# Turned activation blocks sent through DRAM, turns ordered behind residual sums, and a last output tile computed by halves, in a four-layer attention/MLP kernel

## The chip, the cores and the metric

The kernel runs on one core of one Trainium2 chip. The metric is device microseconds of one execution. The kernel before takes 790.73 us (median of three runs: 789.31, 790.73, 791.21).

## The reference, cut to what matters

Four layers run one after the other on the same rows x (2048 tokens of D = 576 features), with the weights of A used twice and those of B used twice:

```
x = A_x
x = x + _A_ref(_layernorm(x), A_wqkv, A_wo)                    # layer 0
x = x + _B_ref(_layernorm(x), B_w1, B_b1, B_w2, B_b2)          # layer 1
x = x + _A_ref(_layernorm(x), A_wqkv, A_wo)                    # layer 2
x = x + _B_ref(_layernorm(x), B_w1, B_b1, B_w2, B_b2)          # layer 3

_A_ref: q,k,v = x@wqkv (32 heads of 18);  pq, pk = phi(q), phi(k);  kv = pk^T v;  z = sum pk
        o = (pq kv) / (pq z + 1e-6);  return o @ wo
_B_ref: y = _layernorm(x);  h = gelu(y@w1 + b1)  (4608 wide);  return h@w2 + b2
```

`_B_ref` normalizes its input once more; the kernel folds the two normalizations into one factor.

## The kernel before, in words

Tokens are cut into 16 tiles of 128 (`t`) and four chunks of 512 (`c`, four tiles each). Every projection wants the normalized rows with features on partitions, so the kernel keeps one big tile `yT` (128 partitions x 5 blocks of features x 2048 tokens): the last block is half full, and for the MLP its 64 rows are there twice, because the MLP works on the two halves of TensorE's rows at once.

**The way into `yT`.** Class `LNPipe` moves one token tile one stage further at each `tick()` (L255): load the rows from the DRAM copy `x_d` into one of two buffers (L265), statistics (L272, L273), `rstd` on GpSimd (L288), normalize into one of three `y_ring` buffers (L307), for the MLP copy the 64 tail columns once more (L311, GpSimd), then turn. Tiles of layer 0 and the first chunk of each MLP are turned on TensorE into a PSUM bank (`tp`, L322 to L328). All others go through `turn_rows` (L221): VectorE turns 32x32 blocks into the one buffer `turned` (L225), which holds the four tiles of a chunk, and after the fourth tile 16 DMAs of 40 or 32 KB each carry the blocks into `yT`, issued from SyncE's queue (L232). The next chunk's first turn overwrites `turned`, so it waits until those DMAs have landed.

**The MLP** (`LayerB.run`, L646). For each chunk: nine groups of the first matmul (`m1_group`, L583; 36 PSUM results through gelu on ScalarE), during which the four tiles of the next chunk are fed to the pipe (`feed_next`, L649); then for each of the four token tiles 72 matmuls of the second projection into one of two PSUM accumulators, `accA` and `accB` (L672), and a residual sum on VectorE (L379) that also frees the accumulator. The first projection of a chunk needs its columns of `yT`. In layer 1 each finished tile is fed to the pipe again, for layer 2. `feed_next` holds loads and statistics behind the last residual sum only for the first chunk.

**The attention layers** (`layer_A`, L388): k and v per tile, q per group of heads and chunk; then denominators (L496, with a one-row matmul that adds epsilon, L500), the scaling (L512 to L515) and the output projection (L523), with the same residual sum.

**What sets the order.** TensorE's order in the program is written out by hand (`pe`, L137). On VectorE, GpSimd and the DMA queue of SyncE a scheduler places the instructions by their dependencies; edges marked NOSYNC only say what stands behind what on one engine. Each engine then works strictly in that order, and an instruction that waits holds all behind it. PSUM has eight banks: three for the pool `ps_h`, one for `tp`, two for each accumulator.

Of the kernel before, what the change touches and what calls it, by code (L numbers as in the profile page):

```python
# [8 lines left out]
ALU = mybir.AluOpType  # L9
BF16 = mybir.dt.bfloat16  # L10
F32 = mybir.dt.float32
PSUM = bass.MemoryType.PSUM
# [3 lines left out]
P = 128  # L16
NT = S // P
KD = 5
# [16 lines left out]
def build(tc, A_x, A_wqkv, A_wo, B_w1, B_b1, B_w2, B_b2, out, dbg=None, n_layers=4):  # L35
    nc = tc.nc
    dbg = dbg or {}
    with ExitStack() as ctx:
        const = ctx.enter_context(tc.tile_pool(name="const", bufs=1))
        ps_h = ctx.enter_context(tc.tile_pool(name="ps_h", bufs=3, space=PSUM))  # L40
        ps_tp = ctx.enter_context(tc.tile_pool(name="ps_tp", bufs=1, space=PSUM))
        ps_acc = ctx.enter_context(tc.tile_pool(name="ps_acc", bufs=1, space=PSUM))
        dpool = ctx.enter_context(tc.tile_pool(name="dram", bufs=1, space=DRAM))

# [172 lines left out]
        state = dict(ycnt=0, vcnt=0, xl=0)  # L217
        pool_last = dict(norm=None)
        dve_last = dict(norm=None, sum=None, phi=None)

        def turn_rows(y, t, kind):  # L221

            c, j = divmod(t, TPC)
            nb = 4 * KD if kind == "B" else D // 32
            nc.vector.transpose(out=turned[:, 0:nb, j, :], in_=y[:, 0:32 * nb])  # L225
            if j < TPC - 1:
                return
            for i in range(4):
                for jj in range(4):
                    nk = KD if 16 + jj < nb else KD - 1  # L230
                    cols = slice(c * CB + i * P, c * CB + (i + 1) * P)
                    nc.sync.dma_start(  # L232
                        out=yT[32 * jj:32 * (jj + 1), 0:nk, cols],
                        in_=turned[32 * i:32 * (i + 1), jj:4 * (nk - 1) + jj + 1:4].rearrange("p k t c -> p k (t c)"))

        def spread(ap):

# [5 lines left out]
        class LNPipe:  # L243
# [9 lines left out]
                return len(self.items)  # L253

            def tick(self, transposes=1):  # L255
                for it in list(self.items):
                    st = it["stage"]
                    if st == 4 and it["evac"] != "dma":
# [27 lines left out]
                    elif st == 1:  # L286
                        rstd = work.tile([P, 1], F32, name="ln_rstd", bufs=6)
                        nc.gpsimd.tensor_tensor(out=rstd[:], in0=it["u"][:], in1=neg_half[:], op=ALU.pow)  # L288
                        it["rstd"] = rstd
                    elif st == 2 and it["norm"] != "dve":  # L290
                        nmr = work.tile([P, 1], F32, name="ln_nmr", bufs=4)
                        nc.gpsimd.tensor_scalar(out=nmr[:], in0=it["mv"][:, 0:1], scalar1=-1.0,
                                                scalar2=it["rstd"][:, 0:1], op0=ALU.mult, op1=ALU.mult)
                        it["nmr"] = nmr
                    elif st in (2, 3):
                        y = y_ring[state["ycnt"] % NY]
                        state["ycnt"] += 1
                        xt = it["xt"]
                        if it["norm"] == "act":
                            nc.scalar.activation(out=y[:, 0:D], in_=xt[:, 0:D], func=ACT.Identity,  # L300
                                                 scale=it["rstd"][:, 0:1], bias=it["nmr"][:, 0:1])
                        elif it["norm"] == "pool":
                            norm = nc.gpsimd.tensor_scalar(out=y[:, 0:D], in0=xt[:, 0:D], scalar1=it["rstd"][:, 0:1],
                                                           scalar2=it["nmr"][:, 0:1], op0=ALU.mult, op1=ALU.add)
                            pool_last["norm"] = norm.ins.name
                        else:
                            norm = nc.vector.tensor_scalar(out=y[:, 0:D], in0=xt[:, 0:D], scalar1=it["mv"][:, 0:1],  # L307
                                                           scalar2=it["rstd"][:, 0:1], op0=ALU.subtract, op1=ALU.mult)
                            dve_last["norm"] = norm.ins.name
                        if it["kind"] == "B":  # L310
                            nc.gpsimd.tensor_copy(out=y[:, D:DPAD], in_=y[:, 4 * P:D])  # L311
                        it["y"] = y
                        it["stage"] = 4
                        continue
                    elif st == 4:
                        y = it["y"]
                        t = it["t"]
                        if it["evac"] == "dma":
                            turn_rows(y, t, it["kind"])
                            self.items.remove(it)  # L320
                            continue
                        tp = ps_tp.tile([P, KD, P], BF16, name="tp", tag="tp")  # L322
                        for k in range(KD):
                            pe(nc.tensor.transpose(out=tp[:, k, :], in_=y[:, k * P:(k + 1) * P], identity=ident[:]))
                        if it["evac"] == "act":
                            nc.scalar.copy(out=yT[:, :, t * P:(t + 1) * P], in_=tp[:])
                        else:
                            nc.vector.tensor_copy(out=yT[:, :, t * P:(t + 1) * P], in_=tp[:])  # L328
                        self.items.remove(it)
                        continue  # L330
                    it["stage"] = st + 1

            def drain(self):
                while self.items:
                    self.tick()

        lnp = LNPipe()
# [34 lines left out]
        def residual(li, t, halves):  # L372
            xo = xo_of.pop((li, t))
            last = (li == n_layers - 1)
            if last:
                xn = work.tile([P, 2 * D], BF16, name="xbf", tag="xn", bufs=3)[:, 0:D]
            else:
                xn = work.tile([P, D], F32, name="xn", tag="xn", bufs=3)[:]
            total = nc.vector.tensor_tensor(out=xn.rearrange("p (h n) -> p h n", h=2), in0=halves,  # L379
                                            in1=xo.rearrange("p (h n) -> p h n", h=2), op=ALU.add)  # L380
            dve_last["sum"] = total.ins.name
            if last:
                nc.sync.dma_start(out=out_f[t * P:(t + 1) * P, :], in_=xn)
                return None
            nc.sync.dma_start(out=x_d[t], in_=xn)
            return xn
# [188 lines left out]
        class LayerB:  # L575
# [70 lines left out]
            def run(self):  # L646
                li, next_kind = self.li, self.next_kind

                def feed_next(c, i):  # L649
                    if c + 1 < NCB:  # L650
                        t = (c + 1) * TPC + i
                        lnp.feed(None, t, "B", "dve", "dma", load_from=t, after=(dve_last["sum"] if c == 0 else None))

                for c in range(NCB):
                    for g in range(self.done.get(c, 0), NGRP):
# [11 lines left out]
                    for j in range(TPC):  # L667
                        t = c * TPC + j
                        acc = ps_acc.tile([P, 2, 512], F32, name="m2_ps", tag=next_acc())
                        for f in range(NF):  # L670
                            for half in range(2):
                                pe(nc.tensor.matmul(acc[:, half, 0:HALF], lhsT=hT[f][:, j * P:(j + 1) * P],  # L672
                                                    rhs=w2_sb[:, f, half * HALF:(half + 1) * HALF],
                                                    start=(f == 0), stop=(f == NF - 1)))
# [111 lines left out]
```

## Time and profile before

The profile is of one execution of 790.27 us; its span is 788.6 us, and 1.67 us lie around the span. Stages by the chain of waits and the timeline:

| stage | span, us | what TensorE does |
|---|---|---|
| layer 0 (attention) | 0 to 112.2 | projections to 75, scaling and output to 112 |
| layer 1 (MLP) | 112.2 to 394.0 | four times 35 us first, 35.4 us second projection |
| layer 2 (attention) | 394.0 to 491.9 | as layer 0 |
| layer 3 (MLP) | 491.9 to 784.9 | first chunk ends late, the others as in layer 1 |
| last sum and store | 784.9 to 788.6 | idle |

| engine | busy us | share of span |
|---|---|---|
| TensorE matmul | 769.9 | 98% |
| ScalarE | 341.7 | 43% |
| VectorE | 275.4 | 35% |
| GpSimd | 127.0 | 16% |

How to read the lines further below: in a timeline a line has start, length, engine, line of the kernel, operation, output<-input with shapes, how many, and in brackets the idle time before it with what ended it. "SPq" is the queue on which SyncE issues DMAs. In the list of waits the numbers are microseconds in total, times, and the longest. In the table of stretches each engine has its busy time and number of instructions; the three last columns are TensorE's granted clock (1.00 is full), the busy share of the DMA engines, and GB/s.

### The profile page before, as it was taken

The numbers are of one execution on the slowest core, as the hardware profiler recorded it, in microseconds if no ns is written. First come the engines' busy times: TensorE is split into PE (matmuls) and PEld (weight loads), VectorE is DVE, ScalarE is ACT, GpSimd is POOL, SyncE is SP. The second block draws the span as 40 slices with busy tenths as digits, with TensorE's granted clock in tenths as the row PEclk, the third lists the DMA queues.
The fourth block names the chain that finished last, engine by engine and source line by source line (L and its number), as shares of the span: only waits on it lengthen the run. The fifth ranks groups of instructions, "written<-read, shape, count | busy, mean of one in ns | idle before, by whom it ended". The sixth has DMA issues, their size and how long they took to land.

```text
span 788.6 us, 15939 instructions
## 1 busy us (share of the span) xinstructions
PE 769.9 (98%) x6613; PEld 496.5 (63%) x6613; DVE 275.4 (35%) x710; ACT 341.7 (43%) x754; POOL 127.0 (16%) x211
## 2 busy tenths in 40 slices
PE   8999999999999999999999999996999999999998
PEld 5776654675477457547777756455744764675476
DVE  6786864044324413301355597544100000000000
ACT  5888636304610650362077774650056016304600
POOL 4671403013000301200000022311110010001000
PEclk9999999999999999999999999998899999999999
DMA  9990473122412331311120028443410110011000
GB/s 265 280 294 5 130 252 91 22 75 66 94 43 69 83 65 46 91 17 31 61 61 2 1 89 288 152 94 79 86 39 1 31 61 2 5 50 38 1 24 23
DMA packets 70642, 63.23 MB, mean 80 GB/s; under 512 B 37418, under 2 KB 55210, under 8 KB 70570
## 3 DMA queue, kind: packets, MB, share of 16 engines
q1 hardware_dynamic: 70570, 62.21, 28.1%
q8 instruction: 52, 0.85, 0.4%
q14 instruction: 20, 0.16, 0.1%
HBM read 39.38 MB, written 16.52 MB: 71 GB/s over the span
## 4 chain that ended last, share of the span: by engine, by line
PE 83%; DVE 7%; DMA 4%; SPq 3%; POOL 1%; issue 1%; ACT 1%; DVEq 0%; POOLq 0%
PE m_ps L672 34%; PE h_ps L624 17%; PE hp_ps L624 14%; PE q_ps L436 5%; PE k_ps L400 5%; PE v_ps L415 3%; SPq L232 3%; PE v_ps L412 2%; PE wo_ps L523 2%; DVE xn L379 1%; DMA x_d<-xn 1%; DVE turned L225 1%; PE kvacc L430 1%; DMA x_ring<-x_d 1%; DVE y_ring L307 1%
## 5 line engine op out<-in xcount | busy, mean ns | idle before, releaser
L672 PE MATMUL m_ps<-w_sb,hT 128*128 128x288 bf16 x2304 | 286.2, 287 | 8.5 <-DVE xbf L379 8.5
L672 PEld LDWEIGHTS <-hT 128*128 128x128 bf16 x2304 | 225.9, 98 | 69.8 <-issue 12.1
L624 PEld LDWEIGHTS <-w_sb 64*128 64x128 bf16 x2304 | 124.4, 94 | 136.6 <-issue 1.9
L624 PE MATMUL hp_ps<-yT,w_sb 64*128 64x512 bf16 x1152 | 178.0, 376 | 0.0
L629 ACT COPY relay_sb<-relay_sb 128x1 f32<-128x1 f32 x144 | 28.5, 198 | 276.6 <-PE h_ps L624 234.7
L624 PE MATMUL h_ps<-yT,w_sb 64*128 64x512 bf16 x1152 | 147.9, 376 | 0.0
L620 ACT ACTIVATE hT<-h_ps,b1T 128x512 bf16<-128x512 f32 x144 | 91.2, 684 | 44.5 <-PE h_ps L624 44.5
L288 POOL TENSOR_TENSOR ln_rstd<-ln_u,neg_half 128x1 f32<-128x1 f32 x64 | 36.2, 567 | 413.9 <-DVE ln_u L281 216.8
L620 ACT ACTIVATE hT<-hp_ps,b1T 128x512 bf16<-128x512 f32 x144 | 91.2, 693 | 0.0
L379 DVE TENSOR_TENSOR xbf<-m_ps,x_ring 128x576 bf16<-128x576 f32 x16 | 12.0, 754 | 221.2 <-PE m_ps L672 221.2
L369 POOL TENSOR_TENSOR x_ring<-x_ring,b_bc 128x576 f32<-128x576 f32 x32 | 41.1, 1291 | 203.7 <-DMA x_ring<-x_d 203.6
L379 DVE TENSOR_TENSOR xn<-m_ps,x_ring 128x576 f32<-128x576 f32 x16 | 12.1, 758 | 155.9 <-PE m_ps L672 155.9
L624 PE MATMUL h_ps<-yT,w_tail 64*128 64x512 bf16 x144 | 54.1, 376 | 0.0
L624 PE MATMUL hp_ps<-yT,w_tail 64*128 64x512 bf16 x144 | 54.1, 376 | 0.0
L436 PE MATMUL q_ps<-yT,wqkv_sb 128*126 128x512 bf16 (+1 forms) x200 | 50.0, 382 | 0.5 <-ACT phi_a L351 0.5
L225 DVE STREAM_TRANSPOSE turned<-y_ring 128x640 bf16<-128x640 bf16 (+1 forms) x40 | 32.2, 812 | 41.8 <-DMA yT<-turned 35.4
L523 PE MATMUL wo_ps<-kvwo,pq 126*128 126x288 bf16 (+1 forms) x320 | 43.7, 285 | 2.1 <-DVE xn L379 1.6
L400 PE MATMUL k_ps<-wqkv_sb,yT 128*128 128x288 bf16 x320 | 44.3, 286 | 0.0
L350 ACT ACTIVATE phi_e<-k_ps 128x288 bf16<-128x288 f32 x64 | 27.0, 421 | 34.8 <-PE k_ps L400 34.7
L352 DVE TENSOR_SCALAR phi_e<-phi_e 128x288 bf16<-128x288 bf16 (+2 forms) x104 | 30.7, 296 | 25.3 <-ACT phi_e L350 24.9
L523 PEld LDWEIGHTS <-pq 126*128 126x128 bf16 (+1 forms) x320 | 30.5, 97 | 13.7 <-issue 3.9
L400 PEld LDWEIGHTS <-yT 128*128 128x128 bf16 x320 | 30.9, 98 | 11.1
(90 smaller groups left out, 625.7 us busy)
## 6 DMA issues: line engine op xcount, KB each, us to landing
x_ring<-x_d SPq DMA_DIRECT2D x72, 288.0 KB, 3.1
x_d<-xn SPq DMA_DIRECT2D x48, 288.0 KB, 2.2
w_sb<-in_B_w_dram SPq DMA_DIRECT2D x6, 864.0 KB, 9.5
yT<-turned SPq DMA_DIRECT2D x128, 40.0 KB, 2.0
w_sb<-in_B_w_dram SPq DMA_DIRECT2D x9, 512.0 KB, 5.5
x<-in_A_x_dram SPq DMA_DIRECT2D x16, 144.0 KB, 4.1
x_ring<-in_A_x_dram SPq DMA_DIRECT2D x16, 144.0 KB, 3.4
out_dram<-xbf SPq DMA_DIRECT2D x16, 144.0 KB, 1.8
```

The costliest lines, as they stand in the source:

```text
L225: nc.vector.transpose(out=turned[:, 0:nb, j, :], in_=y[:, 0:32 * nb])
L288: nc.gpsimd.tensor_tensor(out=rstd[:], in0=it["u"][:], in1=neg_half[:], op=ALU.pow)
L352: nc.vector.tensor_scalar(out=e[0:rows, 0:n], in0=e[0:rows, 0:n], scalar1=1.0, scalar2=1e-6, op0=ALU.min, op1=ALU.add)
L369: nc.gpsimd.tensor_tensor(out=xo, in0=xo, in1=b2_bc[:], op=ALU.add)
L379: total = nc.vector.tensor_tensor(out=xn.rearrange("p (h n) -> p h n", h=2), in0=halves, in1=xo.rearrange("p (h n) -> p h n", h=2), op=ALU ...
L400: pe(nc.tensor.matmul(kp[:, 0:HALF], lhsT=yT[:, k, tok], rhs=wqkv_sb[:, k, D + half * HALF: D + (half + 1) * HALF], start=(k == 0), stop=( ...
L436: pe(nc.tensor.matmul(qp[0:GR[g], :], lhsT=wqkv_sb[:, k, GO[g]:GO[g] + GR[g]], rhs=yT[:, k, c * CA:(c + 1) * CA], start=(k == 0), stop=(k ...
L523: pe(nc.tensor.matmul(wp[:, half, 0:HALF], lhsT=pq[(g, c)][0:GR[g], j * P:(j + 1) * P], rhs=kvwo[g][0:GR[g], half * HALF:(half + 1) * HALF ...
L620: act_last["gelu"] = nc.scalar.activation(out=to, in_=ps, func=ACT.Gelu_apprx_tanh, bias=b1T[:, f:f + 1], scale=1.0).ins.name
L624: mm = pe(nc.tensor.matmul(dst[n], lhsT=wt, rhs=mv, start=(seen[n] == 0), stop=(seen[n] == 8)))
L629: relay = nc.scalar.copy(out=relay_sb[:, 1:2], in_=relay_sb[:, 0:1])
L672: pe(nc.tensor.matmul(acc[:, half, 0:HALF], lhsT=hT[f][:, j * P:(j + 1) * P], rhs=w2_sb[:, f, half * HALF:(half + 1) * HALF], start=(f == ...
```

## The change

- `turn_rows` sends a full `turned` buffer to one of two DRAM buffers `y_d` by four DMAs of 32 x 18 x 128 elements (144 KB each). A list `landing` counts three ticks; then `land` reads the chunk from DRAM into `yT` by one DMA of 128 x 4 x 512 elements and one or, for the MLP, two of 64 x 512. The second of these writes the doubled tail, so the GpSimd copy is left out for these tiles, and 18 instead of 20 blocks are turned.
- Each turn is ordered behind the latest residual sum, and the loads and statistics of all chunks, not of the first alone, behind the latest residual sum at their feeding.
- `tp` has no bank of its own any more; `ps_h` has four banks, `tp` among their users.
- The epsilon matmul has 126 rows (125 of them zero) instead of one.
- The last token tile of the last layer runs its 72 matmuls half by half; the residual sum and the store of that tile are two each, of 288 columns.

```diff
-        ps_h = ctx.enter_context(tc.tile_pool(name="ps_h", bufs=3, space=PSUM))
-        ps_tp = ctx.enter_context(tc.tile_pool(name="ps_tp", bufs=1, space=PSUM))
+        ps_h = ctx.enter_context(tc.tile_pool(name="ps_h", bufs=4, space=PSUM))
...
-        eps_row = const.tile([1, H], BF16, name="eps_row")
-        one_row = const.tile([1, P], BF16, name="one_row")
+        eps_row = const.tile([126, H], BF16, name="eps_row")
+        one_row = const.tile([126, P], BF16, name="one_row")
...
-            fill(eps_row, 1e-6),
+            fill(eps_row, 0.0),
+            lambda: nc.gpsimd.memset(eps_row[0:1, :], 1e-6),
...
-        turned = const.tile([P, 4 * KD, TPC, 32], BF16, name="turned")
+        turned = const.tile([P, D // 32, TPC, 32], BF16, name="turned")
+        y_d = [dpool.tile([D // 32, 32, CB], BF16, name=f"y_d{i}") for i in range(2)]
...
         def turn_rows(y, t, kind):
             c, j = divmod(t, TPC)
-            nb = 4 * KD if kind == "B" else D // 32
-            nc.vector.transpose(out=turned[:, 0:nb, j, :], in_=y[:, 0:32 * nb])
+            turn = nc.vector.transpose(out=turned[:, :, j, :], in_=y[:, 0:D])
+            if dve_last["sum"] is not None:
+                tc.add_manual_dep(turn.ins, dve_last["sum"], NOSYNC, reason="rows are turned behind the sums")
             if j < TPC - 1:
                 return
+            home = y_d[state["turns"] % 2]
+            state["turns"] += 1
             for i in range(4):
-                for jj in range(4):
-                    nk = KD if 16 + jj < nb else KD - 1
-                    cols = slice(c * CB + i * P, c * CB + (i + 1) * P)
-                    nc.sync.dma_start(
-                        out=yT[32 * jj:32 * (jj + 1), 0:nk, cols],
-                        in_=turned[32 * i:32 * (i + 1), jj:4 * (nk - 1) + jj + 1:4].rearrange("p k t c -> p k (t c)"))
+                nc.sync.dma_start(out=home[:, :, i * P:(i + 1) * P].rearrange("j r n -> r j n"),
+                                  in_=turned[32 * i:32 * (i + 1), :, :, :].rearrange("r j t c -> r j (t c)"))
+            landing.append([3, home, c, kind])
+
+        def land(now=False):
+            for it in list(landing):
+                it[0] -= 1
+                if it[0] > 0 and not now:
+                    continue
+                _, home, c, kind = it
+                landing.remove(it)
+                cols = slice(c * CB, (c + 1) * CB)
+                nc.sync.dma_start(out=yT[:, 0:KD - 1, cols],
+                                  in_=home[0:16, :, :].rearrange("(k jj) r n -> (jj r) k n", jj=4))
+                for hi in range(2 if kind == "B" else 1):
+                    nc.sync.dma_start(out=yT[64 * hi:64 * (hi + 1), KD - 1, cols],
+                                      in_=home[16:18, :, :].rearrange("jj r n -> (jj r) n"))
...
             def tick(self, transposes=1):
+                land()
...
-                        if it["kind"] == "B":
+                        if it["kind"] == "B" and it["evac"] != "dma":
                             nc.gpsimd.tensor_copy(out=y[:, D:DPAD], in_=y[:, 4 * P:D])
...
-                        tp = ps_tp.tile([P, KD, P], BF16, name="tp", tag="tp")
+                        tp = ps_h.tile([P, 512], F32, name="tp", tag="h")
+                        tp = tp[:, 0:DPAD // 2].bitcast(BF16).rearrange("p (k n) -> p k n", k=KD)
...
+            parts = [slice(h * HALF, (h + 1) * HALF) for h in range(2)] if last and t == NT - 1 else [slice(0, D)]
+            for i, cols in enumerate(parts):
+                ps = halves if len(parts) == 1 else halves[:, i:i + 1, :]
...
+                if last:
+                    nc.sync.dma_start(out=out_f[t * P:(t + 1) * P, cols], in_=xn[:, cols])
...
-                        lnp.feed(None, t, "B", "dve", "dma", load_from=t, after=(dve_last["sum"] if c == 0 else None))
+                        lnp.feed(None, t, "B", "dve", "dma", load_from=t, after=dve_last["sum"])
...
-                        for f in range(NF):
-                            for half in range(2):
-                                pe(nc.tensor.matmul(acc[:, half, 0:HALF], lhsT=hT[f][:, j * P:(j + 1) * P],
+                        by_half = li == n_layers - 1 and t == NT - 1
+                        steps = [(f, half) for half in range(2) for f in range(NF)] if by_half else \
+                            [(f, half) for f in range(NF) for half in range(2)]
```

More of the change, by code (lines that the diff above doesn't have):

```diff
@@ L215, in build @@
                       [(lambda i=i: piece_w2(i)) for i in range(6)] + [piece_b1_dma]
-        state = dict(ycnt=0, vcnt=0, xl=0)
+        state = dict(ycnt=0, vcnt=0, xl=0, turns=0)
         pool_last = dict(norm=None)
         dve_last = dict(norm=None, sum=None, phi=None)
+        landing = []
         def turn_rows(y, t, kind):
             c, j = divmod(t, TPC)
-            nb = 4 * KD if kind == "B" else D // 32
-            nc.vector.transpose(out=turned[:, 0:nb, j, :], in_=y[:, 0:32 * nb])
+            turn = nc.vector.transpose(out=turned[:, :, j, :], in_=y[:, 0:D])
+            if dve_last["sum"] is not None:
+                tc.add_manual_dep(turn.ins, dve_last["sum"], NOSYNC, reason="rows are turned behind the sums")
             if j < TPC - 1:
                 return
+            home = y_d[state["turns"] % 2]
+            state["turns"] += 1
             for i in range(4):
-                for jj in range(4):
-                    nk = KD if 16 + jj < nb else KD - 1
-                    cols = slice(c * CB + i * P, c * CB + (i + 1) * P)
-                    nc.sync.dma_start(
-                        out=yT[32 * jj:32 * (jj + 1), 0:nk, cols],
-                        in_=turned[32 * i:32 * (i + 1), jj:4 * (nk - 1) + jj + 1:4].rearrange("p k t c -> p k (t c)"))
+                nc.sync.dma_start(out=home[:, :, i * P:(i + 1) * P].rearrange("j r n -> r j n"),
[14 more added lines that the diff above has]
+                                      in_=home[16:18, :, :].rearrange("jj r n -> (jj r) n"))
         def spread(ap):
@@ L325, in tick @@
                         if it["evac"] == "act":
-                            nc.scalar.copy(out=yT[:, :, t * P:(t + 1) * P], in_=tp[:])
+                            nc.scalar.copy(out=yT[:, :, t * P:(t + 1) * P], in_=tp)
                         else:
-                            nc.vector.tensor_copy(out=yT[:, :, t * P:(t + 1) * P], in_=tp[:])
+                            nc.vector.tensor_copy(out=yT[:, :, t * P:(t + 1) * P], in_=tp)
                         self.items.remove(it)
@@ L333, in drain @@
             def drain(self):
-                while self.items:
+                while self.items or landing:
                     self.tick()
@@ L378, in residual @@
                 xn = work.tile([P, D], F32, name="xn", tag="xn", bufs=3)[:]
-            total = nc.vector.tensor_tensor(out=xn.rearrange("p (h n) -> p h n", h=2), in0=halves,
-                                            in1=xo.rearrange("p (h n) -> p h n", h=2), op=ALU.add)
-            dve_last["sum"] = total.ins.name
+            parts = [slice(h * HALF, (h + 1) * HALF) for h in range(2)] if last and t == NT - 1 else [slice(0, D)]
+            for i, cols in enumerate(parts):
+                ps = halves if len(parts) == 1 else halves[:, i:i + 1, :]
+                nh = ps.shape[1]
+                total = nc.vector.tensor_tensor(out=xn[:, cols].rearrange("p (h n) -> p h n", h=nh), in0=ps,
+                                                in1=xo[:, cols].rearrange("p (h n) -> p h n", h=nh), op=ALU.add)
+                dve_last["sum"] = total.ins.name
+                if last:
+                    nc.sync.dma_start(out=out_f[t * P:(t + 1) * P, cols], in_=xn[:, cols])
             if last:
-                nc.sync.dma_start(out=out_f[t * P:(t + 1) * P, :], in_=xn)
                 return None
@@ L669, in run @@
                         acc = ps_acc.tile([P, 2, 512], F32, name="m2_ps", tag=next_acc())
-                        for f in range(NF):
-                            for half in range(2):
-                                pe(nc.tensor.matmul(acc[:, half, 0:HALF], lhsT=hT[f][:, j * P:(j + 1) * P],
-                                                    rhs=w2_sb[:, f, half * HALF:(half + 1) * HALF],
-                                                    start=(f == 0), stop=(f == NF - 1)))
+                        by_half = li == n_layers - 1 and t == NT - 1
+                        steps = [(f, half) for half in range(2) for f in range(NF)] if by_half else \
+                            [(f, half) for f in range(NF) for half in range(2)]
+                        for f, half in steps:
+                            pe(nc.tensor.matmul(acc[:, half, 0:HALF], lhsT=hT[f][:, j * P:(j + 1) * P],
+                                                rhs=w2_sb[:, f, half * HALF:(half + 1) * HALF],
+                                                start=(f == 0), stop=(f == NF - 1)))
+                            if half == 0:
+                                continue
                             if f % 12 == 6:
```

## The prediction

> **What bounds the kernel now.** I read the page's busy times first, then the list of waits, then the place where TensorE waits longest, engine by engine.
>
> The page, engines over the span:
>
> ```profile
> PE 769.9 (98%) x6613; PEld 496.5 (63%) x6613; DVE 275.4 (35%) x710; ACT 341.7 (43%) x754; POOL 127.0 (16%) x211
> ```
>
> TensorE has matmuls in flight all but 18.7 us, so only what it waits for can be won. The list of waits:
>
> ```profile
> DVE turned L225 <- DMA yT<-turned: 35.4, 4, 10.3
> ...
> PE m_ps L672 <- DVE xbf L379: 8.5, 1, 8.5
> ```
>
> One wait of TensorE is long: a second-projection tile waits for a residual sum. The timeline of TensorE around it:
>
> ```profile
> 526.98 17.81 PE L672 MATMUL m_ps<-w_sb,hT 128*128 128x288 bf16 x144
> 553.34 20.19 PE L672 MATMUL m_ps<-w_sb,hT 128*128 128x288 bf16 x144 [8.54 <-DVE xbf L379]
> ```
>
> Two tiles (144 matmuls) of layer 3's first chunk fill both accumulators; the third waits 8.54 us. VectorE at that time:
>
> ```profile
> 537.14 0.58 DVE L307 TENSOR_SCALAR y_ring<-x_ring,ln_mv,ln_rstd 128x576 bf16<-128x576 f32 x1 [0.67 <-POOL ln_rstd L288]
> 545.42 1.57 DVE L225 STREAM_TRANSPOSE turned<-y_ring 128x640 bf16<-128x640 bf16 x2 [7.70 <-DMA yT<-turned]
> ...
> 551.80 0.84 DVE L225 STREAM_TRANSPOSE turned<-y_ring 128x640 bf16<-128x640 bf16 x1 [0.34 <-POOL y_ring L311]
> 552.57 1.38 DVE L379 TENSOR_TENSOR xbf<-m_ps,x_ring 128x576 bf16<-128x576 f32 x2
> ```
>
> The first tile's products lay ready at 526.98 + 17.70/2 = 535.8, but the sum stands in VectorE's order behind the turning of chunk 4, which waits 7.70 us until the DMAs of chunk 3 have left `turned`. Those are slow to issue; SyncE's queue:
>
> ```profile
> 532.80 10.98 SPq L232 DMA_DIRECT2D yT<-turned  x16
> ```
>
> The stretches show the second half of the price, the clock:
>
> ```profile
> 515.00:545.00 30.00, 29.80 (x256) 19.36 (x253) 11.46 (x30) 9.97 (x22) 4.12 (x11) 1.00 0.40 82
> 545.00:560.00 15.00, 6.66 (x35) 4.49 (x35) 7.45 (x16) 0.00 (x0) 1.53 (x4) 0.66 0.29 66
> ```
>
> The granted clock is 0.66 over the stretch with the stall, 1.00 before, and the 144 matmuls behind it take 20.19 us. Undisturbed, 288 take 35.39 us in the chain of waits, so 144 take 17.70: 2.49 us are lost to the clock.
>
> **The change, part by part.** All against the profiled execution, 790.27 us (span 788.6 and 1.67 around it).
>
> 1. *The order on VectorE.* In the changed program's order of instructions, the four sums of layer 3's first chunk stand ahead of all statistics and turns of chunk 3, and those of each later chunk likewise. Only chunk 2 is turned before the first sum; before, it was done by 512.7, and the sum is due at 535.8. So the stall goes whole: −8.54 us, and −2.49 us of slow clock with it. What is late next? Behind 553 TensorE shows no wait before the end, and layer 1 has none at all, although VectorE waits there 10.30 us at 201.6 and 9.53 us at 271.2 for the same reason: the next sum was far away.
>
> 2. *The way through DRAM.* Per chunk 16 issues (10 to 11 us of queue) become 4 writes, one read and one or two tail reads. The trace has no write of 256-byte pieces into DRAM; call W the time from the first of the four issues to the last landing. From below: 288 KB of `x_d<-xn` land in 2.2 us, so 576 KB in 4.4. From above: `yT<-turned`, in equal 256-byte pieces, has 160 pieces per DMA, lands in 2.0 us and is issued every 0.65 us; the 2304 pieces at that pace take 9.4 us and a landing, 11.4; one DMA after the other, 14.4 x 2.0 = 28.8. I take W = 7 us: four issues of about 0.95 (between 0.60 for 160 pieces here and 1.12 for 768 at L196) and some 3 to land, nearer the pipelined row, since the DMAs do overlap in the trace. The read is 512 KB in 1 KB pieces like the `w_sb` loads at L188: 0.6 to issue, 5.5 to land, with the tails 6.5 us.
>
>    Is it hidden? Due times are the starts of the first projection. Layer 1, chunk 2: turned at 131.6, due 182.6. Layer 1, chunks 3 and 4 are tightest, since two sets pass one `turned`: the finished rows' writes start at 188.65, about 7 us of turning follows (201.6 to 208.9) behind their landing, then a second W and the read: 188.65 + 2W + 13.5 against 253.1, so W may be 25.5. Layer 2, tile 12: turned at 398.8, due 435.07 less 6.5: W up to 29.8. Layer 3: chunk 2 from 512.8, due about 562.4; chunks 3 and 4 are now begun only when the chunk before is summed, so load to turn some 16 us (496.9 to 512.7), then 13.5: 30 us of the 70 that a chunk lasts. At W = 7 nothing shows: 0 us. On SyncE's queue the read stands directly behind the writes and holds the queue until they have landed; behind it stand the stores and prefetches of the next chunk's sums, due at about 226 in layer 1, when the queue is free since about 216. The three ticks set program order alone.
>
> 3. *GpSimd's tail copy and two blocks less per turn.* 24 copies (0.25 us) and 24 times some 0.08 us of VectorE go, off the path: 0 us.
>
> 4. *PSUM banks and epsilon rows.* In the attention layers' output stages TensorE waits 0.5 us for a bank (q_ps on ScalarE) and 0.7 (rden_ps on VectorE); four shared banks may save up to 1.2. Four epsilon matmuls advance TensorE 0.19 us in the chain, twenty of the 126-row ones 0.40; at that pace eight groups save 8 x 0.11 = 0.9. A loss is possible where `tp` now keeps a bank of the shared four until ScalarE has copied it: I allow one more wait like that of q_ps, 0.5. In layer 0's first stage each step takes exactly four banks, so each is reused one step later, as before. These stages are VectorE's (16.1 of 17 us busy at 75 to 92), so little reaches the end: −0.3 us, between −2.1 and +0.5.
>
> 5. *The last tile by halves.* The order of matmuls changes, not their number. In the built program the first half's sum waits for TensorE's count of all 6613 matmuls, and the second sum has no wait of its own: TensorE reports once for the tile. So nothing overlaps. Now:
>
> ```profile
> 781.80 3.10 PE L672 MATMUL m_ps<-w_sb,hT 128*128 128x288 bf16 x24
> 785.00 0.76 DVE L379 TENSOR_TENSOR xbf<-m_ps,x_ring 128x576 bf16<-128x576 f32 x1 [8.06 <-PE m_ps L672]
> 785.79 0.33 SPq L383 DMA_DIRECT2D out_dram<-xbf  x1
> ```
>
>    A 288-column row of VectorE (the statistics) takes 0.46 us and starts its successor 0.37 later. The halves end at 785.46 and 785.83 instead of 785.76, and the second issue follows at about 785.9: +0.1 us. Bounds: −0.2 (half the bytes land sooner) to +0.4 (a whole issue more).
>
> Sum: 788.6 − 8.54 − 2.49 − 0.3 + 0.1 = 777.4; with 1.67 around it 779.0. The profiled run is 0.46 below the median of the runs shown, so I forecast 779.3 us, between the two readings. Its own range, from the bounds of 4 and 5 and the runs' spread: 777 to 781.
>
> **The rivals.**
>
> *Slower: the writes into DRAM run one after the other.* Two W must pass in layer 1, chunks 3 and 4; from W = 25.5 on TensorE waits at 253 and 323. At the serial bound, 28.8, each loses 2 x 3.3 = 6.6 us, and 2.5 us of clock as behind the stall here: 2 x 9.1 = 18.2, and 779.3 + 18.2 = 797.5. The gain of 11 us and 2.4 more (0.3%) are given back from 2 x (2 x (W − 25.5) + 2.5) = 13.4 on, at W = 27.6. For it: pieces of 256 bytes, no such row in the trace. Against: sixteen DMAs of such pieces overlapped in 11 us. Chance 0.04. The Trainium skill, "DMA: Bandwidth & Descriptors", sections "Specifications" and "Why small descriptors are slow (HBM only)", speaks for it: transfers under 512 bytes make the engine read, modify and write, and the penalty is on DRAM, not between on-chip memories. If that doubled the 9.4 us of pieces, W would be an estimated 21 us and the sum unchanged.
>
> *No change: the stall moves.* Layer 3's chunks 3 and 4 used to be turned by 533 and 553, 111 and 162 us ahead of their first projections (643.99, 714.45); now the work starts only 70 us ahead. If it took 75 us instead of 30, two stalls of 5 us would give back the gain: 789.3. Against: load to turn of chunk 2 took 16 us with the same instructions. That the order stays as it was is excluded by the listing. Chance 0.05.
>
> *More: part 4 reaches the end.* If its waits lie on the path, another 1.8 us: 777.2. VectorE's 95% speaks against. Chance 0.13.
>
> **How the numbers follow.** Forecast 0.78, more 0.13, stall moves 0.05, serial writes 0.04. A measurement of this kernel can tell about 0.3% (2.4 us) from no change. Faster by over that: 0.91 (the first two); within: 0.05; slower: 0.04. The range, 776.5 to 782.5, holds the first two cases and a little of a stall left over.
>
> **What would show it.** In the changed profile: no TensorE wait at L672's successor before the last sum; VectorE's waits of turns on DMAs (35.4 us) shrunk to the two in layer 1; granted clock 1.00 between 515 and 575; the last two sums both after the last matmul; first projections of layer 1 starting at 182.6, 253.1 and 323.5 as before. A first-projection matmul or a `k_ps` weight load waiting on a DMA would make the forecast wrong, and its length minus 6.5 us of reading gives W.

## The result

The changed kernel takes 778.39 us (median of four runs, 777.95 to 779.44) against 790.02 for the kernel before beside it (four runs, 789.22 to 791.21): ratio 0.9854, 95% interval 0.9835 to 0.9872. The profiled execution took 778.56 us with a span of 776.8. The forecast was 779.3 us.

The page after: engines over the span, and the granted clock of TensorE in 40 slices.

```profile
PE 766.6 (99%) x6613; PEld 495.1 (64%) x6613; DVE 273.3 (35%) x711; ACT 340.6 (44%) x754; POOL 121.4 (16%) x188
PEclk9999999999999999999999999999999999999999
```

TensorE is idle for 10.2 us instead of 18.7, and the clock never drops. The list of TensorE's waits has no row for `m_ps` any more; this is the longest that is left:

```profile
PE wo_ps L548 <- DVE xn L403: 1.8, 4, 0.9
```

The second projection of layer 3's first chunk, on TensorE's timeline, is one block of four tiles:

```profile
526.43 35.45 PE L699 MATMUL m_ps<-w_sb,hT 128*128 128x288 bf16 x288
```

VectorE at that time: the last turn of chunk 2, and behind it nothing but sums, each waiting for TensorE and not the reverse.

```profile
510.10 0.78 DVE L227 STREAM_TRANSPOSE turned<-y_ring 128x576 bf16<-128x576 bf16 x1
535.46 0.76 DVE L403 TENSOR_TENSOR xbf<-m_ps,x_ring 128x576 bf16<-128x576 f32 x1 [24.58 <-PE m_ps L699]
544.28 0.76 DVE L403 TENSOR_TENSOR xbf<-m_ps,x_ring 128x576 bf16<-128x576 f32 x1 [8.06 <-PE m_ps L699]
```

SyncE's queue: a set of four writes into DRAM, and 5.0 us after the first of them the read into `yT`.

```profile
510.91 2.44 SPq L235 DMA_DIRECT2D y_d<-turned  x4
515.92 0.38 SPq L248 DMA_DIRECT2D yT<-y_d  x1
```

The same two stretches as before the change: clock 1.00 in both, and 124 matmuls instead of 35 in the second.

```profile
515.00:545.00 30.00, 30.00 (x260) 19.81 (x255) 1.48 (x2) 9.29 (x21) 1.28 (x1) 1.00 0.14 40
545.00:560.00 15.00, 15.00 (x124) 11.97 (x123) 0.79 (x2) 0.00 (x0) 0.00 (x0) 1.00 0.13 40
```

Where the time came from, as starts on TensorE's timeline (us):

| point | before | after | gained so far |
|---|---|---|---|
| layer 1, first matmul | 112.10 | 110.77 | 1.33 |
| layer 2, first matmul | 393.84 | 392.50 | 1.34 |
| layer 3, first matmul | 491.91 | 491.36 | 0.55 |
| layer 3, second projection of its first chunk | 526.98 | 526.43 | 0.55 |
| layer 3, first projection of chunk 2 | 573.47 | 561.81 | 11.66 |
| last matmul ends | 784.90 | 773.25 | 11.65 |
| span ends | 788.57 | 776.85 | 11.72 |

Of the 11.7 us, 11.11 come from one chunk of layer 3; the rest is some half microsecond in the attention layers and 0.07 behind the last matmul. That layer 2 seems to give back 0.79 us is scatter: from its first matmul to that of layer 3 it takes 98.1 to 99.1 us in the four profiles without the new banks and epsilon rows (the kernel before and three experiments below) and 97.6 to 99.3 in the seven with both whose TensorE has no long wait in layer 1.

### The profile page after: what moved, and what is told of

Read it like the earlier page. It is cut to its first block, busy times and chain, and to the rows that moved or that the text cites. A ratio compares the mean times of both kernels' runs of the same rounds, so it can differ in the third digit from the quotient of the medians.

```text
span 776.8 us, 15765 instructions
## 1 busy us (share of the span) xinstructions
PE 766.6 (99%) x6613; PEld 495.1 (64%) x6613; DVE 273.3 (35%) x711; ACT 340.6 (44%) x754; POOL 121.4 (16%) x188
## 4 chain that ended last, share of the span: by engine, by line
PE 91%; DVE 3%; DMA 2%; POOL 1%; ACT 1%; issue 1%; SPq 0%; DVEq 0%; POOLq 0%; ACTq 0%
PE m_ps L699 36%; PE h_ps L649 20%; PE hp_ps L649 16%; PE k_ps L425 5%; PE q_ps L461 5%; PE v_ps L440 3%; PE v_ps L437 2%; PE wo_ps L548 2%; DVE xn L403 1%; DMA x_d<-xn 1%; PE kvacc L455 1%; DMA wqkv_sb<-in_A_wqkv_dram 1%; POOL y_ring L322 1%; PE tp L344 1%; DMA x<-in_A_x_dram 0%
## 5 line engine op out<-in xcount | busy, mean ns | idle before, releaser
L403 DVE TENSOR_TENSOR xbf<-m_ps,x_ring 128x576 bf16<-128x576 f32 (+1 forms) x17 | 12.2, 721 | 218.5 <-PE m_ps L699 218.5
L649 PEld LDWEIGHTS <-w_tail 64*128 64x128 bf16 x288 | 27.1, 94 | 17.1
```

The lines of the kernel that those rows point to most:

```text
L403: total = nc.vector.tensor_tensor(out=xn[:, cols].rearrange("p (h n) -> p h n", h=nh), in0=ps, in1=xo[:, cols].rearrange("p (h n) -> p h n ...
L649: mm = pe(nc.tensor.matmul(dst[n], lhsT=wt, rhs=mv, start=(seen[n] == 0), stop=(seen[n] == 8)))
```

## The experiments

The theory, as in the prediction: the order on VectorE removes the stall, the way through DRAM costs nothing and gives nothing. Its rival: the stall goes because the DRAM way empties `turned` sooner, and the order is decoration. All ratios are to the kernel before on the same chip, with 95% intervals; that kernel's medians were 790.0 to 790.9.

### The order alone, and the DRAM way alone

`x1_order_only`, the kernel before with only:

```diff
+            turn = nc.vector.transpose(out=turned[:, 0:nb, j, :], in_=y[:, 0:32 * nb])
+            if dve_last["sum"] is not None:
+                tc.add_manual_dep(turn.ins, dve_last["sum"], NOSYNC, reason="rows are turned behind the sums")
...
-                        lnp.feed(None, t, "B", "dve", "dma", load_from=t, after=(dve_last["sum"] if c == 0 else None))
+                        lnp.feed(None, t, "B", "dve", "dma", load_from=t, after=dve_last["sum"])
```

> The kernel before with nothing but the order: turns behind the latest residual sum, loads and statistics of all chunks behind it; the 16 DMAs straight into yT stay. Theory A (the prediction's: the 8.54 us wait and 2.49 us of slow clock come from the order on VectorE, so the order alone suffices): no TensorE wait before the third second-projection tile of layer 3, clock 1.00 there, 11.0 us off the time of the kernel before (about 779.0 us), the attention stages as in the kernel before. Theory B (the slow way out of the buffer is what matters, the order only helps): a wait of several microseconds remains or moves to the first projections, and at most half of the 11 us goes.

Measured: 780.06 us (779.48 to 780.76), ratio 0.9871 (0.9857 to 0.9886).

`x2_dram_only`, the kernel before with only `y_d`, the four writes, `land` and its ticks, 18 blocks turned and no GpSimd tail copy for these tiles; no new edge:

> The kernel before with nothing but the way through DRAM (four writes, one read, one or two tail reads; no tail copy on GpSimd), the sums of layer 3's first chunk still behind the turns of chunks 3 and 4. Theory A in its strict form (the order is the cause): the sum is still late, a TensorE wait of at least 3 us stays, 5 us or less are won. Theory B: a chunk's buffer is free some 6 us after its last turn instead of 13, twice, so VectorE reaches the sum at about 537 to 540 instead of 552.6; it is needed by 544.7, so the wait is gone too and the time is within 1 us of the order alone, about 779 us. If both runs lose the wait, either half of the change was enough by itself.

Measured: 780.04 us (779.41 to 780.58), ratio 0.9871 (0.9856 to 0.9885). The same gain.

VectorE's timeline in `x1_order_only` (turning still by 16 DMAs): the first sum is no longer behind chunks 3 and 4.

```profile
537.02 0.76 DVE L381 TENSOR_TENSOR xbf<-m_ps,x_ring 128x576 bf16<-128x576 f32 x1 [23.71 <-PE m_ps L674]
```

VectorE's timeline in `x2_dram_only`: the old order, all turns of chunks 3 and 4 ahead of the sum.

```profile
518.40 1.44 DVE L227 STREAM_TRANSPOSE turned<-y_ring 128x576 bf16<-128x576 bf16 x2 [0.52 <-DMA y_d<-turned]
...
531.05 1.43 DVE L227 STREAM_TRANSPOSE turned<-y_ring 128x576 bf16<-128x576 bf16 x2
...
537.78 0.78 DVE L227 STREAM_TRANSPOSE turned<-y_ring 128x576 bf16<-128x576 bf16 x1
538.49 0.72 DVE L400 TENSOR_TENSOR xbf<-m_ps,x_ring 128x576 bf16<-128x576 f32 x1
```

Here the sum still stands behind the turns of two chunks, but these hardly wait for DMAs any more. From the first issue of chunk 2's DMAs to the next chunk's turn it is 518.40 − 513.10 = 5.3 us; in the kernel before it was 525.32 − 512.77 = 12.6. Two sets lie ahead of the sum, so it comes 2 x 7.3 = 14.6 us sooner; measured against the first issue, 39.8 us became 25.4, 14.4 sooner. With the sum at 538.49 and TensorE needing the accumulator at 528.03 + 17.7 = 545.7, 6.5 us are to spare. In both kernels the 288 matmuls of this chunk take 35.45 us. So both the theory in its strict form and its rival fall: the two halves of the change each remove the stall by themselves, one by taking the wait away from in front of the sum, the other by making it short enough. Together they remove it once.

### The whole change without the DRAM way

`x6_no_dram`: the edges of `x1_order_only`, the four shared banks and the epsilon rows, with the old turn and a whole last tile.

> The kernel before with the order behind the sums, the four shared banks and the epsilon rows, but with the old turn of 16 DMAs straight into yT and the last tile whole. Theory (the order is enough and the DRAM way adds nothing beside it): 780.1 (order alone) less 0.9 (banks and rows alone) = 779.2, within 0.6 of the changed kernel's 778.4. Rival (the DRAM way is worth something of its own beside the order): clearly above 779.8.

Measured: 778.50 us (777.65 to 779.02), ratio 0.9846 (0.9831 to 0.9861), the changed kernel's time. Beside the order, the DRAM way adds nothing that can be measured.

### A longer way through DRAM

`x_writes4`, and `x_writes8` with `range(8)` in the place of the first `range(4)` of the new line: the changed kernel with

```diff
-            for i in range(4):
+            for i in [i for _ in range(4) for i in range(4)]:
                 nc.sync.dma_start(out=home[:, :, i * P:(i + 1) * P].rearrange("j r n -> r j n"),
```

> The changed kernel with the four writes of a chunk into DRAM issued four times over (16 DMAs to the same place, same data). In the changed kernel's trace a set of four takes 5.0 to 5.9 us from first issue to last landing; each repeat waits for the landing of the one before it to the same place, so I expect W = 13 to 18 us here. Theory (the order on VectorE shields the sums, and the way through DRAM has slack up to W = about 26 us, by 2W + 13.4 before the first projection of layer 1's chunk 3): no TensorE wait, 778.4 us within 0.5. Rival (the short W of the DRAM way is itself what removed the stall): W is again that of the old turn, 13.4 us or more, so the wait for the sum is back, about 11 us, 789.

Measured: 779.41 us (779.19 to 779.45), ratio 0.9858 (0.9841 to 0.9874), W = 14.8 to 15.3 us (first write to the read behind the last landing) in nine of the ten sets; in one the read stands behind other issues, 18.9 us after the first write. SyncE's queue in layer 3:

```profile
512.11 12.42 SPq L235 DMA_DIRECT2D y_d<-turned  x16
526.88 0.38 SPq L248 DMA_DIRECT2D yT<-y_d  x1
```

TensorE shows no wait for it: the order holds the sums free at a W beyond the old one. Of the 1.0 us above the changed kernel, 0.9 are there when layer 3 begins (492.22 against 491.36); in six other profiles with the same attention stages that point lies between 490.39 and 492.41, so this is scatter.

> The changed kernel with the four writes of a chunk into DRAM issued eight times over. W should come out at 23 us if the 32 issues of 0.61 us set the pace and at about 33 if each set of four waits for the landing of the one before. Theory (slack up to W = 26 in layer 1): nothing at W = 23; at W = 33 TensorE waits for yT at the first projections of layer 1's chunks 3 and 4, 2 x (33 - 26) = 14 us each at most, and about 3 us in layer 2, with some 2.5 us of slow clock behind each, 790 to 820. Rival (writes can be stretched without end because of the three steps between write and read): 778.4.

Measured: 835.60 us (834.37 to 836.43), ratio 1.0568 (1.0552 to 1.0584), W = 27.2 to 29.2 us in layer 1. TensorE waited twice, the longest row of its list:

```profile
PE h_ps L649 <- DMA yT<-y_d: 49.7, 2, 28.2
```

The two waits, 28.20 us at 280.9 and 21.55 at 375.6, are 49.7 of the 57 us lost; behind them the granted clock is 0.50 for 5.3 and 2.8 us, and it is 0.969 over the span. By the prediction's formula W = 27.2 should have cost 2 x (27.2 − 25.5) = 3.4 us each and 2.5 of clock. Why so much more? VectorE in layer 1:

```profile
226.25 0.76 DVE L403 TENSOR_TENSOR xn<-m_ps,x_ring 128x576 f32<-128x576 f32 x1 [36.60 <-PE m_ps L699]
226.92 0.77 DVE L227 STREAM_TRANSPOSE turned<-y_ring 128x576 bf16<-128x576 bf16 x1
```

and SyncE's queue:

```profile
187.03 24.79 SPq L235 DMA_DIRECT2D y_d<-turned  x32
...
214.23 0.37 SPq L248 DMA_DIRECT2D yT<-y_d  x1
...
248.73 24.57 SPq L235 DMA_DIRECT2D y_d<-turned  x32
```

`turned` was free at 214.2, but the next set's first turn now stands behind a sum that TensorE delivers at 226.25, and its last behind two more, so the second set of writes starts at 248.73. In the changed kernel it starts at 200.12, 8 us after the read behind the first set. With the repeats the scheduler put the sums first: a long W did not only add its length, the order changed with it. Why the scheduler did so here, and not in `x8_big_pieces` below with as many DMAs, stays open.

### The same repeats without the edges

`x2_writes4`: `x2_dram_only` with each write four times.

> The kernel before with the way through DRAM alone, no order behind the sums, and its four writes issued four times over: W = 13 to 18 us as in the changed kernel with the same repeats. Theory (two halves that each remove the wait: the order whatever W is, the DRAM way only because its W is short): the first sum of layer 3 stands behind two more sets of turning, so it moves from 538.5 to 555 or later and TensorE waits 10 to 25 us for it, with 2.5 us of slow clock: 788 to 808. Rival (the DRAM way removes the wait by something other than its short W, such as the reads being taken out of the wait): 780.0 as with single writes.

Measured: 779.37 us (778.66 to 779.79), ratio 0.9857 (0.9843 to 0.9872). No stall, against the theory's 788 to 808. VectorE's timeline:

```profile
527.72 1.44 DVE L227 STREAM_TRANSPOSE turned<-y_ring 128x576 bf16<-128x576 bf16 x2 [10.49 <-DMA y_d<-turned]
...
539.93 0.75 DVE L400 TENSOR_TENSOR xbf<-m_ps,x_ring 128x576 bf16<-128x576 f32 x1
```

The wait of the turn is back (10.49 us), but the sum now stands ahead of chunk 4's turns, the first of which come at 574.12: the scheduler moved them with no edge to tell it so. It also spread chunk 3's 16 writes among other issues: the first starts at 534.47, the read at 573.99. This run therefore does not test what it was made for, W at a fixed order; that test is the pair of the kernel before and `x2_dram_only` above, whose order of turns and sums is the same.

### Banks and epsilon rows

`x3_banks_eps`: the kernel before with four shared banks and 126 epsilon rows only.

> The kernel before with nothing but the four shared PSUM banks and the 126-row epsilon matmul. Prediction's term: -0.3 us (between -2.1 and +0.5), the 8.5 us wait stays, so about 790.0 us. Rival: the 1.3 us by which layer 1 begins earlier in the profile of the changed kernel (110.77 instead of 112.10) are these edits, and then layer 1 begins at 110.8 here too; the changed kernel's profile lost 0.8 of them again in layer 2's output stage, and if that is theirs as well, layer 3 begins 0.5 us earlier than in the kernel before; if it is chance, 1.3 to 2.6 us earlier.

Measured: 789.58 us (787.12 to 790.57, ten runs), ratio 0.9986 (0.9976 to 0.9997). Then each alone: `x9_eps_only` and `x10_banks_only`.

> The kernel before with only the epsilon rows of 126 partitions. In all profiles with these rows the way from z_ps to the first wo_ps takes 9.12 us instead of 9.53, in layer 0 and in layer 2. Theory (this stretch is TensorE's own pace and its 0.8 us reach the end): ratio about 0.9990, 790.0 where before has 790.8. Rival (the four shared banks give the 0.9 us seen for both together): no change, and 9.53 still.

> The kernel before with only the four shared PSUM banks. Theory (the 0.9 us of both together come from the epsilon rows): 9.53 us from z_ps to the first wo_ps as before, no change of time beyond 0.3 us. Rival (the banks remove waits for q_ps and v_ps, up to 1.2 us): faster by 0.5 to 1.2 us.

Measured: epsilon rows alone 789.91 us, ratio 0.9994 (0.9986 to 1.0003), not told from no change; banks alone 789.05 us, ratio 0.9981 (0.9972 to 0.9990), 1.5 us (0.8 to 2.2) faster. The theory for `x10_banks_only` falls by this time. That for `x9_eps_only` falls by the next figures, not by its time (its 0.9990 lies inside the interval). From `z_ps` to the first `wo_ps` it is 9.53 us in layers 0 and 2 before, 9.41 and 9.43 with the rows alone, 9.20 in both with the banks alone, 9.12 or 9.13 with both. So in this stretch the banks shorten each attention layer by 0.33 us and both edits together by 0.41. In TensorE's list of waits, of the kernel before:

```profile
PE rden_ps L512 <- DVE rden L504: 0.7, 2, 0.3
...
PE q_ps L436 <- ACT phi_a L351: 0.5, 2, 0.2
```

Neither row is left with the banks alone, nor after the change: together 1.2 us. But a new row stands in every profile with the four banks and in none without them; after the change it is

```profile
PE wo_ps L548 <- DVE kvwo L511: 0.9, 2, 0.5
```

So most of what the banks remove there comes back as a wait for other work of VectorE, and the list of waits alone does not explain 1.5 us. Part of that figure may be the stall of layer 3, which all these kernels still have: from second to next first projection it lasts 46.49 us in the profile before, 45.37 with the banks alone, 47.24 with the rows alone and 45.24 with both. Two measures are free of it. Layer 3's first matmul starts at 491.9 to 493.0 us in the four profiles without both edits and at 490.4 to 492.4 in the seven with both, 1.0 us earlier in the mean; and `x6_no_dram` is 1.6 us below `x1_order_only` in the medians, from which it differs by these two edits alone (they ran on different chips). What the rows alone are worth stays open; it is under 1.1 us.

### The last tile by halves

`x4_two_tiles`: the changed kernel, whose last tile's second half goes into an accumulator of its own.

```diff
+                        second = ps_h.tile([P, 512], F32, name="m2_half", tag="h") if by_half else None
...
-                            pe(nc.tensor.matmul(acc[:, half, 0:HALF], lhsT=hT[f][:, j * P:(j + 1) * P],
+                            pe(nc.tensor.matmul(second[:, 0:HALF] if by_half and half else acc[:, half, 0:HALF], lhsT=hT[f][:, j * P:(j + 1) * P],
```

> The changed kernel with the second half of the last output tile in a PSUM tile of its own, so that the first half's sum has its own count to wait for. Theory A (the halves overlap nothing while they share one tile, because TensorE reports once per tile): the first half's sum now starts some 4.4 us before the last matmul ends, one sum of about 0.45 us is left behind it, and the span ends 0.3 to 0.4 us earlier than the changed kernel's 776.8. Rival: the end is set by the landing of the last store alone, and nothing changes.

Measured: 778.40 us (777.91 to 778.74), ratio to before 0.9849 (0.9833 to 0.9866), the changed kernel's time. VectorE after the change, and then with two accumulators:

```profile
773.35 0.82 DVE L403 TENSOR_TENSOR xbf<-m_ps,x_ring 128x288 bf16<-128x288 f32 x2 [8.06 <-PE m_ps L699]
```

```profile
769.34 0.46 DVE L403 TENSOR_TENSOR xbf<-m_ps,x_ring 128x288 bf16<-128x288 f32 x1 [3.65 <-PE m_ps L700]
773.69 0.46 DVE L403 TENSOR_TENSOR xbf<-m_half,x_ring 128x288 bf16<-128x288 f32 x1 [3.90 <-PE m_half L700]
```

With one accumulator both sums run after the last matmul, at 773.35; with two the first runs 4.3 us ahead. Behind the last matmul come 3.7 us before the change, 3.6 after it and 3.1 with two accumulators: half a microsecond, which the spread of the runs covers.

`x7_best`, `x6_no_dram` with these true halves, is the smallest program that has all that showed a gain.

> The kernel with the order, the banks and the epsilon rows, the old turn of 16 DMAs, and the last tile by halves with a second accumulator of its own. In the profile of the changed kernel with two accumulators the first half's sum started at 769.34, ahead of the last matmul at 773.65, and 3.05 us followed that matmul; with one whole tile and the old turn 3.6 us followed it. Theory (the halves can overlap only where each has its own accumulator): 3.05 us behind the last matmul, 778.5 less 0.55 = 778.0 us, too little to be told from 778.5 by time alone. Rival (the second store's landing sets the end whatever is ahead): 3.6 us and 778.5.

Measured: 778.30 us (777.60 to 778.47), ratio 0.9839 (0.9827 to 0.9852); 3.2 us behind the last matmul. It is not told from the changed kernel, but has no way through DRAM.

### What pieces of 256 bytes cost

`x8_big_pieces`: the changed kernel with 28 more writes per chunk, of the bytes that `x_writes8` adds, in pieces of 4608 bytes into a DRAM buffer that nobody reads.

```diff
+            for i in [i for _ in range(7) for i in range(4)]:
+                nc.sync.dma_start(out=big_d[32 * i:32 * (i + 1), :],
+                                  in_=turned[32 * i:32 * (i + 1), :, :, :].rearrange("r j t c -> r (j t c)"))
```

> The changed kernel with 28 more writes per chunk of the same bytes as the extra ones of the kernel with eight sets (147 KB each, from the same 32 partitions), but into DRAM rows of their own, in pieces of 4608 bytes instead of 256. With pieces of 256 bytes 32 writes took 27.2 us, 0.79 us each after the first issues, at a DMA share of 0.95. Theory (pieces under 512 bytes pay a double price on the way into DRAM): a set of 32 takes 13 to 18 us and may be bound by the issuing instead (0.4 to 0.6 us each). Rival (the pieces cost nothing here, the bytes or the 32 partitions set the pace): about 27 us again. The run's time follows from W and from how the planner then orders the turns, between 778 and 840 us.

Measured: 778.42 us (two runs), W = 22.2 to 23.4 us in layer 1, between the theory's 13 to 18 and the rival's 27. A stretch of layer 1 in `x8_big_pieces`, and one in `x_writes8`; the last two columns are the DMA engines' busy share and GB/s:

```profile
187.00:205.00 18.00, 18.00 (x171) 8.08 (x167) 3.79 (x9) 12.03 (x29) 4.80 (x5) 1.00 0.86 252
```

```profile
189.00:211.00 22.00, 22.00 (x208) 9.93 (x204) 0.58 (x1) 15.98 (x35) 0.03 (x1) 1.00 1.00 187
```

Per busy time of the DMA engines that is 252/0.86 = 293 GB/s against 187; over other sets of layer 1 it is 280 to 288 against 178 to 188, so the small pieces cost 1.5 to 1.6 times as much. They also lie 1 KB apart in DRAM, where the large ones lie side by side, and no run separates the two. The large ones are issued every 0.60 us (28 in 16.9 us) and leave the engines idle for 14% of the stretch, so W says less than the rates do. As a test of slack it says that with the order of the changed kernel kept (the second set's writes start at 216.92, ahead of the sum) W of 22 to 23 us still costs nothing.

## Why the prediction was right, step by step

*What bounds the kernel.* Right: the one long wait of TensorE, and the clock behind it, were all that could be won in quantity.

*Step 1, the order.* Stall and clock, 8.54 + 2.49 = 11.03 us: measured 11.11, from the start of the second projection to the next first projection 46.49 us before and 35.38 after. The size was right, the attribution half so. The prediction gave the whole gain to the order and 0 to the DRAM way; the DRAM way alone gains the same, because the old wait was only some 8.5 us too long and that way shortens it by 14.4. It had the numbers for this (W, and two sets ahead of the sum) and worked them out for `yT` only.

*Step 2, the DRAM way.* W was put at 7 us; it is 4.9 to 5.9. Four issues take 2.4 to 2.7 us (once 3.2), 0.6 each and not 0.95: a write with 576 pieces is issued as fast as the old turn's DMA with 160. The 1.12 us taken from L196 was a mean of issues of 0.40, 0.54 and 2.32 us, and so no price of pieces. With W this short VectorE's wait for `turned` is gone in layer 1 too, where two such waits were to remain; they do remain in `x1_order_only` (14.8 us in two). "Hidden, 0 us" was right: `x6_no_dram` lacks the way and has the same time. The limit of slack, W = 25.5, is not contradicted: with the order kept, 22 to 23 us cost nothing. Beyond it the runs do not test it, since the 57 us of `x_writes8` come with another order, which the working held fixed. So the rival of serial writes was rightly held unlikely (four writes take 5 us together), and its price of 18 us stays untested: four slow writes would not have given the scheduler 32 DMAs to place.

*Step 3, the GpSimd copy and fewer blocks.* 0 us; GpSimd's busy time went from 127.0 to 121.4 us with no trace on TensorE's; no run has this part alone.

*Step 4, banks and epsilon rows.* The term that was mis-sized: −0.3 us, measured −1.1 for both (−1.9 to −0.2, by the interval of `x3_banks_eps`) and −1.0 and −1.6 by the two measures above, inside the stated −2.1 to +0.5. The step that failed is "these stages are VectorE's, so little reaches the end": more of it does. It is not a plain sum of waits removed either, since 0.9 of the 1.2 us come back on another row; of the way to the end, 0.8 us are seen between `z_ps` and `wo_ps`, and where the rest arises stays open. A term of −1.0 to −1.6 would account for about the 0.9 us between forecast and measured median; the profile of the changed kernel shows only 0.55 of it, within the scatter. The rival "part 4 reaches the end" had this step better, but its 777.2 is further from 778.39 than the forecast is.

*Step 5, halves.* No overlap, as read from the program; −0.07 us instead of +0.1, within the bounds. `x4_two_tiles` shows the reason (one accumulator, one report) by taking it away.

*The Trainium skill's rule against the change* ("DMA: Bandwidth & Descriptors", "Specifications": transfers under 512 bytes are read, modified and written). Here the pieces of 256 bytes, 1 KB apart, cost 1.5 to 1.6 times the DMA time of large ones, so a penalty exists, but with four writes a chunk the whole set takes 5 us and TensorE does not wait for it. The mechanism is not shown by these runs: that page of the Trainium skill, "Why small descriptors are slow (HBM only)", names a fixed overhead per piece besides, 27% for 256 bytes, which is less than what is seen.

*The stall moves.* It did not: chunks 3 and 4 of layer 3, turned later than before, show no wait.

## What to carry to other kernels

When two parts of a change act on one wait, work out for each alone whether it removes the wait: here each did, and the sum of a change is then the gain of one. A shorter wait and a wait out of the way look the same in the time until the wait is stretched; and where a scheduler orders the queues, stretching it can change the order too, so read the order of each experiment's own trace before believing what it tested. Small waits for banks on the bounding engine can reach the end even in a stage where another engine is busier; but measure the stage as a whole, since a wait that is removed can come back on another row.

## What the runs showed of the hardware

- A stall of 8.54 us of TensorE cost another 2.5 us by the clock: granted clock 0.50 for the first 4.9 us after it and 1.00 from then on, and 144 matmuls took 20.19 us instead of 17.70. The price does not follow the length of the stall: in the other five long waits of these profiles (7.9, 8.1 and 9.4 us with the banks, both edits and the rows; 28.20 and 21.55 in `x_writes8`) the clock stayed at 0.50 for 3.9, 3.4, 4.6, 5.3 and 2.8 us after the wait, half of which is lost, 1.4 to 2.7 us.
- Writes of 256-byte pieces into DRAM, 1 KB apart, move 171 to 188 GB/s with the DMA engines 96 to 100% busy (`x_writes8`); pieces of 4608 bytes side by side 280 to 293 GB/s per busy time (`x8_big_pieces`).
